# Attention, gated FFN and routed experts on one core: weight conversion at one unit a round, the small block's last logits inside the first Strassen group, ScalarE's casts and GpSimd's work moved within a group, another PSUM bank for the first w_out product

## The chip, the core and the metric

The kernel runs on one core of one Trainium2 chip. The metric is the device time of one execution in microseconds (us), the median over several runs. A profile of one execution was taken by the hardware profiler as well. Engines: PE (matrix products; PEld is its loading of the stationary operand), DVE (vector), ACT (scalar, activations and casts), POOL (GpSimd), SP (issues most DMAs).

## The reference

Three layers follow each other, all in 32-bit floats, over 2304 tokens of width 512.

```python
# 1. attention by random features, per batch and head (4 x 8, 576 tokens, width 64, 128 features)
phi(x) = exp(x@omega.T - |x|^2/2 - max) / sqrt(128)      # of q and k, scaled
out = (phi(q) @ (phi(k).T @ v)) / (phi(q) @ phi(k).sum + 1e-6)
# 2. gated FFN, 512 -> 1536 -> 512
xn  = x / sqrt(mean(x*x) + 1e-6) * rms_g
y   = (silu(xn @ w_gate) * (xn @ w_val)) @ w_out
# 3. routing over 8 experts, each takes 288 tokens
logits = y @ w_gate2                        # 2304 x 8
order  = argsort(-logits.flatten())         # greedy: best (token, expert) pairs first
out[mask_e] = relu(y[mask_e] @ w1[e]) @ w2[e]   # 512 -> 1024 -> 512
```

## The kernel before

Every float product is made from two parts: a matrix is cut into a high part in PE's reduced 32-bit format and a low part, the rest, and a product is three matmuls (high x high, low x high, high x low). So each operand costs a cast (ACT, the high part) and a subtraction (DVE or POOL, the low part).

The program runs through these stages; the times in the tables below are from the start of the profiled span.

1. **Rounds of attention** (0 to about 325 us). A round (`run_tick`) starts one item of the attention, K items and Q items in turn, while five older items go on; in between stand steps of the FFN (`ffn_step_pe`) on the token blocks that are ready. Each round also takes up some of 48 *weight units*: 24 units of `w_gate`/`w_val` (`WgvUnit`), 12 of `w_out` transposed (`WoTUnit`) and 12 of `w_out` (`WoUnit`), 512 KB each, which arrive as 64-bit floats and are turned into 32-bit ones by one pass of ACT and three of DVE (`word`, L592 to L594). How many units start a round is `PACE`: 0.5 at first, 0.7 up to the last `WgvUnit`, then its third number.
2. **The small block** (to about 352 us). Tokens come in five blocks of 512, 512, 256, 512 and 512. The third, of 256, is the small block; after the attention, PE makes its products f by f (f is one of 12 slices of the 1536 columns, `KF`), gate (L676 to L679, v = 0) and value (v = 1). ACT and DVE make th and h of them, ACT casts h (L709), POOL makes the low part (L710), and PE multiplies both with the router's weights into the logits' bank `lg` (`ffn_lg`, L721 and L722), one step behind. Between the steps stand preparations for the next stage (the list `ins`). At the end the last logits are made, transposed (`ffn_rank`, L733) and ranked (`ffn_rank_el`), and three matmuls into the PSUM banks bb, bc and bd (L1183) mark these as written.
3. **Groups** (`group(f)`, f = 0 to 12, about 352 to 495 us). Blocks four and five (LEFT and RIGHT) are multiplied together by Strassen's method: seven half products instead of eight, 42 matmuls of 512 columns a group, in this order: pa (bank gv), pe (gv), bb with t2, pa again, bb with t3, bc, bd. ACT copies pa into bb (L1089), pe into p5 (L1102) and bb into bd (L1128). DVE adds bb and p5 into bc (L1109), which has to be there before bb is written again by t3. Beside this stand the logits of LEFT and RIGHT of the group before (`logits_of`), and those of block 0 (`late_lg`), for which h of block 0 is loaded from DRAM two slices ahead (`late_load`, L923), cast by ACT and reduced by POOL (`late_split`: L928, L932) and stored again (L933). The next group's operands are made by `turn_w` (POOL L1008, DVE L1012 to L1015), `turn_high` (ACT L1019) and `turn_low` (POOL L1022). Every second group takes up 1024 columns of w_out: `wo_load` (SP), `wo_high` (ACT), `wo_low` (DVE L903, two halves).
4. **w_out and routing** (about 495 to 672 us). The product with w_out (`ffn2`, 648 matmuls at L1264) is the filling between the steps of the routing (`route`), which DVE and PE do in turns: `fill(ns)` lets PE make so many matmuls of the filling, and after the routing the rest is made. Ahead of the routing stand the last logits of LEFT and RIGHT (`ffn_lg`, `ffn_rank`). The routing's result picks the rows that are gathered for expert 0.
5. **Experts** (to the end).

The order is written by hand: inside `manual_schedule` PE, DVE and ACT (in the groups POOL too) do their instructions in the order of the code; SP's DMAs stand in one queue and each waits for its own inputs with all behind it.

Of the kernel before, what the change touches and what calls it, by code (L numbers as in the profile page):

```python
# [9 lines left out]
F32 = mybir.dt.float32  # L10
# [40 lines left out]
SKIP = 2  # L51
STEP = (1.08, 0.5)
SLOW_AT = 71
PACE = (0.5, 0.7, 0.75)
FFN_AT = 23
AHEAD_A = 200
AHEAD_F = 150
# [238 lines left out]
def kernel(ctx, tc, qT, kT, kC, v1, vC, om, wgv, rms, wo, woT, wg2, w1, w2, cfd, trd, out, dbg=None):  # L296
# [647 lines left out]
    def late_lg():  # L944
        f = late["lg"]
        if f < late["split"]:
            ffn_lg(0, f, lates[f])
            late["lg"] += 1
            if f + 2 < KF:
                late_load(f + 2)  # L950
# [114 lines left out]
    def group(f):  # L1065

        last, nxt = f == KF, f + 1 if f + 1 < KF else None
        if not last:
            w = wsl[f].rearrange("p l (b x) -> p l b x", b=4)
            b11, b21, b22 = ((w[:, 0, i], w[:, 1, i]) for i in (0, 1, 3))  # L1070
            (t1, t3), (t2, t4) = ([(ta[f, n][:, 0, i], ta[f, n][:, 1, i]) for i in range(2)] for n in range(2))
            a11, a12 = ((xlh[:, 2 * i:2 * i + 2], xll[:, 2 * i:2 * i + 2]) for i in (0, 1))
            pa = wide(psG, "gv")
            product(pa, *b11, *a11, True)
        late_lg()
        if not f:
            sum_low("s4", 1, s1[1], nc.vector)
            sum_low("r2", 1, right_2(1), nc.gpsimd)
            late_load(0)
            late_load(1)  # L1080
        if f:
            keep_low(LEFT, f - 1, *old["l"])
            th2 = wide(fp, "th")
            gate(th2, bd)
            times_gate(th2, bd)
            times_value(th2, old["p5"])
            late_split()
        if not last:
            nc.scalar.copy(bb, pa)  # L1089
        if f:  # L1090
            hp2 = pair()
            keep_high(th2, hp2)
        if nxt:
            turn_w(nxt, 1)
        if f:
            keep_low(RIGHT, f - 1, th2, hp2)
        if last:
            return
        pe = wide(psG, "gv")
        product(pe, *t1, *both("s1"), True)  # L1100
        p5 = wide(sp, "p5", bufs=2)
        nc.scalar.copy(p5, pe)  # L1102
        logits_of(LEFT)
        product(bb, *t2, *both("s2"), False)
        if nxt:
            turn_w(nxt, 2)
            turn_high(nxt, 0)
            turn_low(nxt, 0)
        nc.vector.tensor_add(bc_, bb, p5)  # L1109
        if f % 2:  # L1110
            wo_low()
            wo_load(f // 2)
        product(pa, *b21, *a12, False)
        th1 = wide(fp, "th")
        gate(th1, pa)
        times_gate(th1, pa)
        if f + 2 < KF:
            turn_w(f + 2, 0)
            turn_w(f + 2, 5)
        logits_of(RIGHT)  # L1120
        if f % 2 and f > 1:
            late_lg()
            late_split()
        product(bb, *t3, *both("s3"), False)
        if f and not f % 2:
            wo_high()
            wo_low()
        nc.scalar.copy(bd, bb)  # L1128
        nc.vector.tensor_add(p5, bb, p5)
        if nxt:  # L1130
            turn_high(nxt, 1)
            turn_low(nxt, 1)
        ffn_rank()
        product(bc_, *b22, *both("s4"), False)
        hp1 = pair()
        times_value(th1, bc_)
        keep_high(th1, hp1)
        ffn_rank_el(1)
        product(bd, *t4, *both("r2"), False)
        old.update(l=(th1, hp1), p5=p5)  # L1140

    def logits_of(j):
        if fq and fq[0][0] == j:
            ffn_lg(*fq.pop(0))

    dve, pool = nc.vector, nc.gpsimd
# [19 lines left out]
    with tc.manual_schedule(engines=in_order | {mybir.EngineType.Pool}):  # L1166
        count, rounds = len(ready), len(ins)
        while ready:
            el = fst.pop("el", None)
            assert ffn_step_pe()  # L1170
            if el:
                ffn_el(*el)
                ffn_rank_el()
            while len(ins) > rounds * len(ready) // count:
                for make in ins.pop(0):
                    make()
        ffn_step_el()
        while fq:
            ffn_lg(*fq.pop(0))
        ffn_rank()  # L1180
        ffn_rank_el()
        for t in (bb, bc_, bd):
            nc.tensor.matmul(t, xlh[:, 0, :128], xlh[:, 0], start=True, stop=True)  # L1183
    st["rank"] = lambda: psS.tile([128, 512], F32, name="late")[:, :BLK // 128 * 2 * E].rearrange(
        "p (c e) -> p c e", e=2 * E)
    st["eng"] = nc.vector
    with tc.manual_schedule(engines=in_order | {mybir.EngineType.Pool}):
        for f in range(KF + 1):
            group(f)
            if f == KF - 3:  # L1190
                ffn2_load(*seq2[0], x2, "xh2", 1)
                ffn2_load(*seq2[1], x2, "xl2", 1)
        wo_high()
        wo_low()
        wo_low()
# [53 lines left out]
    def ffn2():  # L1249
        for i, (c, g) in enumerate(seq2):  # L1250
            if i + HB - 1 < len(seq2):
                ffn2_load(*seq2[i + HB - 1], f2, "ht", HB)
            if i % 6 == 2 and wcur[0] < LOADS:
                exp_load()
            if i % 6 == 4 and wcur[1] < EARLY:
                exp_early()
            ht = hts.pop((c, g))
            if g == 0:
                py = psB.tile([128, DM], F32, name="py")
            for i4 in range(4):  # L1260
                f = 4 * g + i4
                w = wos[f // 2].rearrange("p l (i d) -> p l i d", i=2)
                for n, (a, l) in enumerate(((0, 0), (0, 1), (1, 0))):
                    nc.tensor.matmul(py, ht[:, i4, a], w[:, l, f % 2], start=(f == 0 and n == 0),  # L1264
                                     stop=(f == KF - 1 and n == 2))
                    yield
            if g == 2:
                done[0] += 1
                t = c - (NC - TAIL)
                if t >= 0:  # L1270
                    for h in (slice(0, 256), slice(256, 512)):
                        nc.scalar.copy(yt[t][:, 0, h], py[:, h])
                        nc.vector.tensor_sub(yt[t][:, 1, h], py[:, h], yt[t][:, 0, h])
                ys = yp.tile([128, DM], F32, name="ys")
                nc.scalar.copy(ys, py)  # L1275
                nc.scalar.dma_start(y_dr[c * 128:(c + 1) * 128, :], ys)
# [15 lines left out]
    with tc.manual_schedule(engines=in_order):  # L1292
        for n in (8, 6):
            fill(n * FILL_MM)
            ffn_lg(*fq.pop(0))
            fill(3 * FILL_MM)
            ffn_rank()
            ffn_rank_el()
    if "L" in dbg:
        nc.sync.dma_start(dbg["L"].rearrange("(c p) e -> p c e", p=128), L)  # L1300
    xg = {}
# [218 lines left out]
```

## Time and profile before

| | |
|---|---|
| time, median of 3 runs | 910.35 us (907.67 to 911.21) |
| profiled execution | 909.13 us, of which the span from first to last instruction is 907.3 us |
| PE busy | 881.3 us, 97% of the span |
| PE weight loads | 763.0 us, 84% |
| DVE busy | 633.5 us, 70% |
| ACT busy | 412.3 us, 45% |
| POOL busy | 259.3 us, 29% |
| mean granted clock of PE | 0.993 |

A busy share is the time in which the engine had an instruction running; matmuls overlap, so that the one recorded end lies behind the start of the next. "Idle before" in a row is time in which the engine stood still ahead of that instruction, with the one that released it.

### The profile page before, as it was taken

Reading aid. Unit: us, or ns where it says so; the run is one execution under the profiler, and the core shown is the slowest. Engines: PE = TensorE matmul, PEld = TensorE weight load, DVE = VectorE, ACT = ScalarE, POOL = GpSimd, SP = SyncE. Lnnn points to the kernel's source line nnn. Section 1 sums busy time; section 2 is a strip of 40 time slices with the busy share of each in tenths; the row PEclk is TensorE's granted clock in tenths of the full one; section 3 lists DMA queues with packets and bytes.
Section 4 is the critical chain, followed back from the end, with each engine's and each line's share of the span. In section 5 each row is a group of like instructions: output and inputs, shape, how many; then the busy total and the mean of one; then the engine's idle time right before and its main releaser. Section 6 shows DMA issues by size and latency. Waiting matters only on the chain.

```text
span 907.3 us, 15714 instructions
## 1 busy us (share of the span) xinstructions
PE 881.3 (97%) x5780; PEld 763.0 (84%) x5780; DVE 633.5 (70%) x1398; ACT 412.3 (45%) x913; POOL 259.3 (29%) x313
## 2 busy tenths in 40 slices
PE   9999999999999988999999999999999999999996
PEld 7788888888888987777776777777779999999996
DVE  4899967577757885788887777777654665556652
ACT  6886666355555743555554101100014454445441
POOL 1355433132322536566651000000022122122211
PEclk9999999999999998999999999999999999999998
DMA  8657435543456223466654987777614566665550
GB/s 303 203 145 223 137 108 160 177 146 120 139 181 233 82 82 120 145 207 218 217 183 164 302 253 211 214 216 210 195 56 127 183 188 190 194 212 180 182 187 27
DMA packets 114109, 159.26 MB, mean 176 GB/s; under 512 B 6640, under 2 KB 71664, under 8 KB 114032
## 3 DMA queue, kind: packets, MB, share of 16 engines
q1 hardware_dynamic: 108224, 143.96, 50.7%
q0 software_dynamic: 3072, 9.44, 3.5%
q10 hardware_dynamic: 2736, 4.85, 1.4%
q8 instruction: 45, 0.74, 0.3%
q14 instruction: 32, 0.26, 0.1%
HBM read 114.19 MB, written 44.04 MB: 174 GB/s over the span
## 4 chain that ended last, share of the span: by engine, by line
PE 46%; issue 8%; DVE 6%; POOL 3%; ACT 1%; DMA 0%; POOLq 0%; ACTq 0%; DVEq 0%
PE py L1264 15%; PE ph L1376 3%; PE ph L1379 3%; PE ph L1377 3%; PE py L1389 3%; PE py L1387 3%; PE py L1388 3%; DVE th L1061 1%; PE bb L1027 1%; PE gv L1030 1%; PE gv L1028 1%; PE gv L1027 1%; PE bb L1028 1%; PE bb L1030 1%; POOL out_dram L1423 1%
## 5 line engine op out<-in xcount | busy, mean ns | idle before, releaser
L1264 PE MATMUL py<-wc,ht 128*128 128x512 f32 x624 | 158.4, 402 | 0.0
L1264 PEld LDWEIGHTS py<-wc,ht 128*128 128x128 f32 x624 | 111.6, 189 | 19.2
L1235 DVE TENSOR_TENSOR wc<-ws,wc 128x512 fp32r<-128x512 f32 x128 | 84.5, 684 | 35.5 <-ACT wc L1245 35.5
L676 PE MATMUL gv<-xh,wc 128*128 128x512 f32 (+1 forms) x288 | 104.6, 374 | 2.4 <-DVE th L689 1.2
L677 PE MATMUL gv<-xh,wc 128*128 128x512 f32 (+1 forms) x288 | 99.4, 356 | 0.0
L409 ACT ACTIVATE ft<-pp,mx 128x128 f32<-128x128 f32 x288 | 82.9, 374 | 30.3 <-DVE mx L406 30.0
L1389 PE MATMUL py<-ehh,wc 128*128 128x288 f32 x256 | 76.2, 298 | 0.0
L1387 PE MATMUL py<-ehh,wc 128*128 128x288 f32 x256 | 75.8, 296 | 0.0
L1388 PE MATMUL py<-ehl,wc 128*128 128x288 f32 x256 | 75.6, 295 | 0.0
L1376 PE MATMUL ph<-exh,wc 128*128 128x288 f32 x256 | 71.2, 300 | 0.0
L1275 ACT COPY ys<-py 128x512 f32<-128x512 f32 x18 | 10.6, 588 | 133.0 <-PE py L1264 108.8
L1377 PE MATMUL ph<-exh,wc 128*128 128x288 f32 x256 | 69.8, 295 | 0.0
L1245 ACT CAST wc<-ws 128x1024 fp32r<-128x1024 f32 x64 | 67.2, 1050 | 2.4 <-ACT ys L1275 2.4
L679 PE MATMUL gv<-xl,wc 128*128 128x512 f32 (+1 forms) x288 | 67.1, 355 | 0.0
L676 PEld LDWEIGHTS gv<-xh,wc 128*128 128x128 f32 x288 | 54.5, 189 | 10.5 <-DVE th L689 2.4
L1381 DVE SCALAR_TENSOR_TENSOR ehl<-ph,ehh 128x288 fp32r<-128x288 f32 x64 | 29.3, 458 | 46.7 <-ACT ehh L1380 42.2
L677 PEld LDWEIGHTS gv<-xh,wc 128*128 128x128 f32 x288 | 54.5, 189 | 6.4
L406 DVE TENSOR_REDUCE mx<-pp 128x4 f32<-128x512 f32 (+1 forms) x76 | 49.9, 657 | 12.2 <-PE pp L402 7.9
L679 PEld LDWEIGHTS gv<-xl,wc 128*128 128x128 f32 x288 | 49.3, 189 | 8.0
L1315 POOL DMA_INDIRECT xh<-y_dr,idc x3 | 3.1, 1038 | 167.9 <-DVE idc L1327 167.3
L1423 POOL DMA_INDIRECT out_dram<-yo,ids x24 | 22.5, 938 | 98.1 <-DVE yo L1418 75.4
L1380 ACT ACTIVATE ehh<-ph 128x288 fp32r<-128x288 f32 x64 | 26.4, 412 | 49.7 <-PE ph L1379 49.7
(305 smaller groups left out, 2223.6 us busy)
## 6 DMA issues: line engine op xcount, KB each, us to landing
ws<-in_w_dram SPq DMA_DIRECT2D x64, 512.0 KB, 4.0
ht<-h_dr SPq DMA_DIRECT2D x53, 512.0 KB, 4.5
h_dr<-hp SPq DMA_DIRECT2D x36, 512.0 KB, 2.8
ws<-in_wgv_dram SPq DMA_DIRECT2D x24, 512.0 KB, 4.3
h_dr<-hp SPq DMA_DIRECT2D x24, 256.0 KB, 3.2
ws<-in_woT_dram SPq DMA_DIRECT2D x12, 512.0 KB, 3.5
ws<-in_wo_dram SPq DMA_DIRECT2D x12, 512.0 KB, 3.7
h_dr<-xh SPq DMA_DIRECT2D x12, 512.0 KB, 3.6
```

The costliest lines, as they stand in the source:

```text
L409: st["ex"] = nc.scalar.activation(ft[:n, g], pp[:n, g], AF.Exp, bias=mx[:n, g:g + 1])
L676: nc.tensor.matmul(pg[:, :n], w[:, 0, v, k], xh[:, k, :n], start=(k == 0), stop=False)
L677: nc.tensor.matmul(pg[:, :n], w[:, 1, v, k], xh[:, k, :n], start=False, stop=False)
L679: nc.tensor.matmul(pg[:, :n], w[:, 0, v, k], xl[:, k, :n], start=False, stop=(k == KD - 1))
L1235: nc.vector.tensor_sub(w[:, 1, h], sv[:, h], w[:, 0, h])
L1245: nc.scalar.copy(w[:, 0], sv)
L1264: nc.tensor.matmul(py, ht[:, i4, a], w[:, l, f % 2], start=(f == 0 and n == 0), stop=(f == KF - 1 and n == 2))
L1376: nc.tensor.matmul(ph, w[:, 0, k, m], xh[:, k], start=(k == 0), stop=False)
L1377: nc.tensor.matmul(ph, w[:, 1, k, m], xh[:, k], start=False, stop=False)
L1387: nc.tensor.matmul(py, w[:, 0, k], hh[:, k], start=(k == 0), stop=False)
L1388: nc.tensor.matmul(py, w[:, 0, k], hl[:, k], start=False, stop=False)
L1389: nc.tensor.matmul(py, w[:, 1, k], hh[:, k], start=False, stop=(k == KE - 1))
```

## The change

Four things are edited.

- `PACE`'s third number goes from 0.75 to 1.0: after the last `WgvUnit`, every round starts a unit.
- The small block's last two slices of logits are no longer made ahead of the groups. `logits_of` takes them too, so that they stand in group 0 where later groups have those of LEFT and RIGHT; their ranking follows in group 0, and the three marking matmuls are moved to where six steps of the small block are left.
- In the groups, `late_lg` stands behind pe and behind the logits of RIGHT (before: behind pa, and in odd groups behind RIGHT); `late_split` behind RIGHT in odd groups and at the end of every group (before: early in every group, and behind RIGHT in odd ones); the first `turn_high`/`turn_low` behind the gate; `wo_high` behind the copy of pe; `wo_low` behind the sum into bc.
- The first product with w_out is made in the bank gv instead of py; the filling between the last logits and their ranking is 4 matmuls (before 3), and 2 more follow the second ranking.

```diff
-PACE = (0.5, 0.7, 0.75)
+PACE = (0.5, 0.7, 1.0)
...
             product(pa, *b11, *a11, True)
-        late_lg()
...
             times_value(th2, old["p5"])
-            late_split()
...
         nc.scalar.copy(p5, pe)
+        if f and not f % 2:
+            wo_high()
+        late_lg()
         logits_of(LEFT)
         product(bb, *t2, *both("s2"), False)
         if nxt:
             turn_w(nxt, 2)
-            turn_high(nxt, 0)
-            turn_low(nxt, 0)
         nc.vector.tensor_add(bc_, bb, p5)
+        wo_low()
         if f % 2:
-            wo_low()
             wo_load(f // 2)
         product(pa, *b21, *a12, False)
...
         times_gate(th1, pa)
+        if nxt:
+            turn_high(nxt, 0)
+            turn_low(nxt, 0)
...
         logits_of(RIGHT)
-        if f % 2 and f > 1:
-            late_lg()
+        late_lg()
+        if f % 2:
             late_split()
         product(bb, *t3, *both("s3"), False)
-        if f and not f % 2:
-            wo_high()
-            wo_low()
...
             turn_high(nxt, 1)
             turn_low(nxt, 1)
+        if f:
+            late_split()
         ffn_rank()
...
     def logits_of(j):
-        if fq and fq[0][0] == j:
+        if fq and fq[0][0] in (j, LEFT - 1):
             ffn_lg(*fq.pop(0))
...
         while ready:
+            if len(ready) == count - 6:
+                for t in (bb, bc_, bd):
+                    nc.tensor.matmul(t, xlh[:, 0, :128], xlh[:, 0], start=True, stop=True)
...
-        while fq:
-            ffn_lg(*fq.pop(0))
-        ffn_rank()
-        ffn_rank_el()
-        for t in (bb, bc_, bd):
-            nc.tensor.matmul(t, xlh[:, 0, :128], xlh[:, 0], start=True, stop=True)
...
-                py = psB.tile([128, DM], F32, name="py")
+                py = psB.tile([128, DM], F32, name="py") if i else psG.tile([128, DM], F32, name="gv")
...
-            fill(3 * FILL_MM)
+            fill(4 * FILL_MM)
             ffn_rank()
             ffn_rank_el()
+        fill(2 * FILL_MM)
```

On PE, at the end of the small block, before: the last logits (lg) stand between the small block's products and in the first product of group 0 (L1027 on, gv from xh).

```order
L679 MATMUL gv<-xl_1913,wc 128x256 x4
L721 MATMUL lg<-hp,wog 16x256
L722 MATMUL lg<-hp,wog 16x256
L721 MATMUL lg<-hp,wog 16x256
L722 MATMUL lg<-hp,wog 16x256
L1027 MATMUL gv<-xh,wc 128x512
L1028 MATMUL gv<-xh,wc 128x512
L1027 MATMUL gv<-xh,wc 128x512
L721 MATMUL lg<-hp,wog 16x256
L1028 MATMUL gv<-xh,wc 128x512
L722 MATMUL lg<-hp,wog 16x256
L1030 MATMUL gv<-xl,wc 128x512 x2
```

And after, from the same place: two products of group 0 follow at once, and the next pair of logits stands behind them.

```order
L679 MATMUL gv<-xl_1915,wc 128x256 x4
L721 MATMUL lg<-hp,wog 16x256
L722 MATMUL lg<-hp,wog 16x256
L1027 MATMUL gv<-xh,wc 128x512
L1028 MATMUL gv<-xh,wc 128x512
L1030 MATMUL gv<-xl,wc 128x512 x2
L1027 MATMUL gv<-s_4004,ta 128x512
L1028 MATMUL gv<-s_4004,ta 128x512
L1030 MATMUL gv<-s_4004,ta 128x512 x2
L721 MATMUL lg<-hp,wog 16x256
L722 MATMUL lg<-hp,wog 16x256
L1027 MATMUL bb<-s_4116,ta 128x512
```

The last pair (not among these rows) stands behind the two products after those, t2 into bb and the second half of pa; both pairs wait for POOL's L710 as before.

On POOL, groups 2 and 3 and the first row of group 4, before (ta is `turn_low`, ws is `turn_w`, xh is the low part of block 0's h):

```order
L932 TENSOR_TENSOR xh<-xh 128x2x256
L1022 TENSOR_TENSOR ta<-dw,ta 128x512
L1008 TENSOR_TENSOR ws<-wc 128x512 x2
L1022 TENSOR_TENSOR ta<-dw,ta 128x512
L932 TENSOR_TENSOR xh<-xh 128x2x256
L1022 TENSOR_TENSOR ta<-dw,ta 128x512
L1008 TENSOR_TENSOR ws<-wc 128x512 x2
L932 TENSOR_TENSOR xh<-xh 128x2x256
L1022 TENSOR_TENSOR ta<-dw,ta 128x512
L932 TENSOR_TENSOR xh<-xh 128x2x256
```

The same groups after:

```order
L1022 TENSOR_TENSOR ta<-dw,ta 128x512
L1008 TENSOR_TENSOR ws<-wc 128x512 x2
L1022 TENSOR_TENSOR ta<-dw,ta 128x512
L932 TENSOR_TENSOR xh<-xh 128x2x256
L1022 TENSOR_TENSOR ta<-dw,ta 128x512
L1008 TENSOR_TENSOR ws<-wc 128x512 x2
L932 TENSOR_TENSOR xh<-xh 128x2x256
L1022 TENSOR_TENSOR ta<-dw,ta 128x512
L932 TENSOR_TENSOR xh<-xh 128x2x256
L1022 TENSOR_TENSOR ta<-dw,ta 128x512
```

The xh of a group's start has moved to its end, behind the second ta, and the first ta starts later in its group, since its cast now stands behind the gate.

On PE, at the start of the filling with w_out, before (num is the bank of the transposed logits):

```order
L1264 MATMUL py<-wc,xh_5281 128x512 x8
L721 MATMUL lg<-hp,wog 16x512
L722 MATMUL lg<-hp,wog 16x512
L1264 MATMUL py<-wc,xh_5281 128x512 x3
L733 MATMUL num<-cf,th 128x16 x4
```

And after:

```order
L1264 MATMUL gv<-wc,xh_5281 128x512 x8
L721 MATMUL lg<-hp,wog 16x512
L722 MATMUL lg<-hp,wog 16x512
L1264 MATMUL gv<-wc,xh_5281 128x512 x4
L733 MATMUL num<-cf,th 128x16 x4
```

The bank is another and one matmul more stands ahead of the ranking; up to the first step of the routing (L188) there are 4 more in all, which are missing from the filling's rest at the end.

## Rows read from the trace of the kernel before

**Rows 1.** The profile's page, part 1: busy time of each engine.

```profile
PE 881.3 (97%) x5780; PEld 763.0 (84%) x5780; DVE 633.5 (70%) x1398; ACT 412.3 (45%) x913; POOL 259.3 (29%) x313
```

**Rows 2.** Windows: busy us of PE, PEld, DVE, ACT, POOL, granted clock, DMA.

```profile
352.00:356.00 4.00, 1.75 (x10) 0.89 (x7) 3.93 (x5) 0.40 (x1) 4.00 (x4) 1.00 0.18 66
356.00:363.00 7.00, 6.54 (x17) 4.79 (x18) 1.64 (x5) 1.90 (x5) 1.33 (x3) 0.51 0.83 241
...
369.00:484.00 115.00, 112.80 (x489) 84.29 (x489) 100.38 (x126) 62.57 (x110) 66.93 (x53) 1.00 0.56 194
```

**Rows 3.** Timeline of PE, last logits to group 1's start: start, us, [idle before].

```profile
352.13 0.28 PE L721 MATMUL lg<-hp,wog 128*16 128x256 f32 x1
353.91 0.29 PE L722 MATMUL lg<-hp,wog 128*16 128x256 f32 x1 [1.50 <-POOL hp L710]
...
356.46 0.39 PE L722 MATMUL lg<-hp,wog 128*16 128x256 f32 x1 [1.22 <-POOL hp L710]
...
369.28 0.39 PE L1027 MATMUL gv<-xh,wc 128*128 128x512 f32 x1
```

**Rows 4.** PE's waits from 280 to 330 us: total, times, longest.

```profile
PE pm L501 <- DVE x L528: 1.4, 1, 1.4
PE pm L511 <- DVE x L528: 1.1, 1, 1.1
PE pm L511 <- DVE xn L551: 0.7, 2, 0.4
```

**Rows 5.** PE's waits from 159 to 280 us.

```profile
PE gv L676 <- DVE th L689: 1.2, 1, 1.2
```

**Rows 6.** DVE's groups, 280 to 330 us: count, busy us, mean ns, idle before.

```profile
L593 DVE SCALAR_TENSOR_TENSOR dw<-ws,dw 128x512 int32<-128x512 int32 x6 | 5.4, 905 | 0.1
L594 DVE SCALAR_TENSOR_TENSOR dw<-ws,dw 128x512 int32<-128x512 int32 x6 | 4.3, 714 | 0.1
L592 DVE TENSOR_SCALAR dw<-dw 128x512 int32<-128x512 int32 x6 | 4.0, 672 | 0.0
```

**Rows 7.** Timeline of PE in group 4, which begins at 403.65.

```profile
403.65 0.39 PE L1027 MATMUL gv<-xh,wc 128*128 128x512 f32 x1
...
410.23 0.39 PE L722 MATMUL lgr<-hp,wog 128*16 128x512 f32 x1
410.92 0.50 PE L1027 MATMUL bb<-xl,ta 128*128 128x512 f32 x1 [0.30 <-DVE bc L1109]
...
415.14 0.39 PE L1027 MATMUL gv<-xh,wc 128*128 128x512 f32 x1
```

**Rows 8.** Timelines of DVE and POOL in group 4.

```profile
403.87 1.12 DVE L1048 TENSOR_TENSOR hp<-th,hp 128x512 fp32r<-128x512 f32 x1 [0.69 <-ACT hp L1045]
405.62 1.32 DVE L1061 SCALAR_TENSOR_TENSOR th<-p,th 128x512 f32<-128x512 f32 x1
...
408.69 1.56 DVE L1015 TENSOR_TENSOR dw<-ws,dw 128x256 f32<-128x256 f32 x1
413.99 0.69 DVE L1061 SCALAR_TENSOR_TENSOR th<-bc,th 128x512 f32<-128x512 f32 x1
405.10 1.30 POOL L932 TENSOR_TENSOR xh<-xh 128x512 fp32r<-128x512 f32 x1 [0.66 <-ACT xh L928]
```

**Rows 9.** DMA issues from 357 to 500 us: count, size, median us to landing.

```profile
h_dr<-xh SPq DMA_DIRECT2D x12, 512.0 KB, 3.6
...
xh<-h_dr SPq DMA_DIRECT2D x10, 256.0 KB, 3.2
```

**Rows 10.** Timelines of PE and DVE around the filling.

```profile
496.51 0.50 PE L1264 MATMUL py<-wc,xh 128*128 128x512 f32 x1 [1.47 <-DVE th L1058]
510.22 0.23 PE L188 MATMUL cnt<-oh,xh 128*128 128x8 bf16 x3 [0.79 <-DVE xh L142]
673.95 0.30 PE L1359 MATMUL gv<-cf,xh 96*128 96x96 f32 x1 [0.91 <-DVE xh L1335]
500.52 0.19 DVE L736 TENSOR_TENSOR L<-num,lt 128x32 f32<-128x32 f32 x1 [0.41 <-ACT lt L735]
```

More of the change, by code (lines that the diff above doesn't have):

```diff
@@ L1177 @@
         ffn_step_el()
-        while fq:
-            ffn_lg(*fq.pop(0))
-        ffn_rank()
-        ffn_rank_el()
-        for t in (bb, bc_, bd):
-            nc.tensor.matmul(t, xlh[:, 0, :128], xlh[:, 0], start=True, stop=True)
-    st["rank"] = lambda: psS.tile([128, 512], F32, name="late")[:, :BLK // 128 * 2 * E].rearrange(
-        "p (c e) -> p c e", e=2 * E)
+        assert len(fq) == 2
     st["eng"] = nc.vector
@@ L1189 @@
             group(f)
+            if f == 0:
+                st["rank"] = lambda: psS.tile([128, 512], F32, name="late")[:, :BLK // 128 * 2 * E].rearrange(
+                    "p (c e) -> p c e", e=2 * E)
             if f == KF - 3:
```

## Prediction

> **What bounds the kernel now.** I read the page's table of engines first, then the windows, then PE's waits and timelines at the places that the diff touches. PE is busy for 881.3 of 907.3 us, DVE for 633.5, ACT and POOL for less [rows 1]: PE is the bound nearly everywhere, so the change can only gain where PE stands still or runs slowly, and a wait that it adds on PE counts in full. The change removes almost no matmuls. The profiled execution took 909.13 us (its span and 1.8 us around it); the median of the runs is 910.35, so I sum against 909.13 and put 0.6 on top, half of the 1.2 between them. No change means within 0.5%, 4.55 us, about what a measurement of this kernel can tell: below 905.8 is faster, above 914.9 slower.
>
> **Part 1, the small block's last logits.** PE goes from the last pair of logits but one (352.13) to the start of group 1 (369.28), 17.15 us in all [rows 3]. Two things make that long. PE waits 1.50 and 1.22 us for POOL's low parts of h, at 353.91 and 356.46 [rows 3]; between 352 and 356 it is busy for only 1.75 of 4.00 us. And from 356 to 363 the granted clock is 0.51, the lower of its two levels, 1.2 instead of 2.4 GHz, right behind those idle stretches, while PE has 6.54 us of work [rows 2].
>
> What is that work at the full clock? In group 4, 29 matmuls of 512 columns lie between 403.65 and 410.23 [rows 7], which is 0.227 us each (with one pair of logits among them, so a little too much is charged to each). Group 0 has 42: 9.55 us. I add two pairs of logits of 256 columns at half of 0.227 per matmul, 0.45, and 0.45 for the transposes with a short wait for their copy: 10.5. The three marking matmuls, 0.7, now stand earlier, but they still cost their time: 11.2. So 17.15 − 11.2 = **−6.0 us**.
>
> Does POOL hold PE up elsewhere? Its low parts are ready where the two waits end, 353.9 and 356.4 [rows 3]. After the change the first six matmuls of pa and six of pe are ahead of the first of these logits: 352.1 + 0.7 + 12 × 0.227 = 355.5, and t2 and the rest of pa ahead of the other: 12 × 0.227 + 0.3 later, 358.5. Both low parts are then there, if POOL isn't later than now, and nothing of what DVE or POOL do ahead of it has grown. Bounds: if the waits go but the clock falls all the same, 1.50 + 1.22 = −2.7; if the transposes need no wait either, −6.4.
>
> **Part 2, PACE.** Between 280 and 330 PE waits 1.4 + 1.1 + 0.7 = 3.2 us, all for x and xn, small operations of DVE's FFN steps [rows 4]; there DVE converts weight units, six words at 5.4 + 4.3 + 4.0 = 13.7 us, 2.3 us each [rows 6], and the FFN's operations stand behind them in DVE's order. 24 units at 0.75 a round take 32 rounds, at 1.0 they take 24; six words from 280 on are eight rounds, and I take a round at 5 us (an estimate, from the 50 us of these rows and the words' end before them), so the last word comes some 40 us earlier, near 279 instead of 319. The stretch with the waits is then nearly free of words. I don't take off all: the second wait has other causes as well, so I count 2.4 of 3.2. The rounds from 159 to 280 get denser in turn, four words where three were; now, with three, PE waits there only 1.2 us for DVE in 121 us [rows 5], so a third more words should add 0.4 to 0.5. Together **−1.9 us**. Bounds: all 3.2 gone and nothing added, with a little less jitter, −3.5; nothing gone, and one wait as long as the 1.4 us above added in the denser rounds, about +1.5.
>
> **Part 3, the order within the groups.** Groups 1 to 10 fill the 115 us from 369 to 484; group 4 takes 415.14 − 403.65 = 11.49 [rows 7]. PE is busy for 112.80 of 115.00 us there, at clock 1.00 [rows 2]. The missing 2.2 us are nearly all one wait: t3's first matmul, which overwrites bb, waits for DVE's sum into bc (0.30 us in group 4, at 410.92) [rows 7]. That is what a better order can give as visible idle; at 0.227 us for each of the 489 matmuls in the window the ten groups would take 111.0 us, so with what the records don't show as idle it is 4.0 at most.
>
> What makes bc late is DVE's chain, hp (L1048), th (L1058, L1061), the differences L1012 to L1015, then bc. Three of its operations are drawn out: L1048 takes 1.12, L1061 1.32 and L1015, with half the columns, 1.56, where an undisturbed L1061 takes 0.69; L1061 falls into POOL's xh of 405.10 to 406.40 [rows 8]. An L1015 without that would take half of 0.69, 0.35, so 0.43 + 0.63 + 1.21 = 2.3 us of the chain are such waiting behind POOL. The Trainium skill says in "SBUF — State Buffer", section "SBUF: two separate sides", that DVE with two inputs in SBUF and a GpSimd operation that reads SBUF exclude each other for a whole instruction, whichever started first; 1.32 against 0.69 agrees, and by that rule POOL's work costs DVE wherever it lands in the chain, so moving it helps only if it leaves the chain.
>
> It leaves it in odd groups only halfway. After the change xh stands at the end of each group, behind the second ta, and the first ta behind the gate. At the start of an even group POOL then still has ws, xh and ta of the change of groups in one run, some 1.3 us each by the row of xh [rows 8], beside DVE's L1048 and L1061: I count one collision more, 2.3 → about 3.2 us. Against this PE itself arrives later at t3 in even groups, since `late_lg`'s second pair now stands ahead of it: 2 × 0.227 = 0.45. So bc is 0.5 to 1.0 later, PE 0.45 later: 0.1 to 0.5 a group in five even groups. In odd groups `late_lg` is unchanged in place, but its low part comes from a later xh: 0 to 0.2. Group 1 has its ranking ahead of bc gone to group 0, worth some 0.5 back. Sum **+1.0 us**. Bounds: −4.0 if the wait for bc vanishes everywhere; +8 by the late loads (a rival below).
>
> **Part 4, filling and routing.** The first product's bank py was the last group's bd, and PE waits 1.47 us at 496.51 for DVE's last reading of it; in gv it need not. But PE is not alone there: the first step of the routing (0.79 at 510.22) waits for DVE's chain from the logits, which starts with L736 behind ACT's copy (0.41) [rows 10]. The matmuls come earlier and PE then waits for DVE, unless the added filling covers it: 4 matmuls more, 0.9 us, are drawn from the end of the filling, where PE waits 0.91 for the gather (673.95) [rows 10] and will wait about 1.8 instead. What stays is by how much DVE's routing starts earlier, at most the 0.41 of that copy: **−0.4 us**. Bounds 0 and −1.5 (1.47 in full).
>
> **Sum.** −6.0 − 1.9 + 1.0 − 0.4 = −7.3; 909.13 − 7.3 = 901.8, and with the 0.6 of the median 902.4: I say **902 us**.
>
> **The rivals.**
>
> *The clock falls all the same* (or at another place). The start of group 0 still has a copy, a transpose and two logits in it, and the gather's wait grows to 1.8 us. One stretch as now costs half of 7.0 us at 0.51 [rows 2], 3.4 us: 902 + 3.4 = 905.5. For it: 2.7 us of idle time sufficed for the fall at 356. Against: after the change no single wait over 0.3 us is in sight there, and the waits for bc in groups 1 to 10, of a few tenths each, left the clock at 1.00 [rows 2].
>
> *The wait for bc goes as well.* If DVE, in even groups, starts its chain before POOL (whose xh now stands at the end), the collisions leave the chain: not +1.0 but −4.0: 897. For it: in odd groups the xh that hit L1061 has moved away. Against: the ta and ws that took its place are as long.
>
> *The late loads pile up: the rival on the other side.* The place is the end of each group. A slice of h is loaded once its store two slices before has landed, 3.6 us after issue, and its own landing takes 3.2 more [rows 9]. With the split at the end of the group the store goes out later, so in odd groups the load may land after ACT has come to the cast L928, and ACT queues hp's cast, the gate and the copy into bb behind it: all that DVE's chain and PE's next group need. Up to 0.65 us of such a wait has slack (ACT is busy for 62.57 of 115 [rows 2]); each tenth above it is a tenth on PE. At 0.85 us a group, 8.5 over ten groups in place of the +1.0, the gain is gone: 902 − 1 + 8.5 = 909.5. From 1.4 us a group on it is 915 and more, slower. For it: 6.8 us of DMA in a loop of 11.49. Against: a slice has two groups, 23 us, and the DMA share there is 0.56 [rows 2].
>
> *PACE does nothing, or shifts the waits into the rounds before:* +0 to +1.5 instead of −1.9, 904 to 905.5.
>
> **How the numbers follow.** The forecast with all its terms, 898 to 905: 0.60. The clock falls somewhere, 904 to 907: 0.13. bc's wait goes too, 895 to 898: 0.12. Late loads or collisions at about one us a group, 908 to 916: 0.15, of which 0.06 is above 914.9. PACE without effect lies inside the first two. Below 905.8 lie the first, the third and a third of the second: 0.76; above 914.9 0.06; between 0.18. Leaving out a small tail on either side, below 895 and above 909, leaves 8 in 10 or a little more.
>
> **What the profile should show.** No wait for POOL at the two pairs of logits, granted clock 1.00 from 350 to 370, and 11 to 11.5 us from the last product of the small block to group 1. No L592 to L594 after about 280, and less than 1 us of waits for x and xn in 280 to 330. Groups 11.3 to 11.8 us long, with PE's wait for bc there and L1048, L1061 or L1015 at 1.1 us and more beside a POOL operation. The first L1264 directly behind bd, and a wait of about 1.8 us for the gather. I am wrong if the granted clock is near 0.5 at group 0, if the groups last 12 us with ACT's L928 waiting for a DMA, or if waits of more than 2 us for DVE appear between 159 and 280.

## The result and the profile after

The changed kernel takes 900.47 us (median of 4 runs, 899.24 to 900.84) where the kernel before takes 909.56 (4 runs): ratio 0.9898, 95% interval 0.9875 to 0.9922, a gain of 9.1 us. The prediction said 902 and a gain of about 8. The profiled execution has a span of 898.8 us, 8.5 less than before.

The page's first part shows that PE's work is the same and its idle time shorter.

```profile
PE 880.0 (98%) x5780; PEld 763.7 (85%) x5780; DVE 626.0 (70%) x1400; ACT 411.3 (46%) x913; POOL 260.8 (29%) x311
```

At group 0 the windows answer to [rows 2]; the last is a stretch behind the gather, which we come back to.

```profile
352.00:356.00 4.00, 4.00 (x20) 3.17 (x19) 2.35 (x4) 1.53 (x4) 0.91 (x2) 1.00 0.54 166
356.00:363.00 7.00, 6.58 (x30) 4.77 (x29) 5.63 (x11) 3.21 (x7) 5.09 (x4) 1.00 0.77 242
369.00:484.00 115.00, 113.69 (x492) 84.62 (x491) 90.45 (x129) 61.43 (x108) 68.94 (x51) 1.00 0.58 202
665.00:675.00 10.00, 10.00 (x69) 9.95 (x69) 3.63 (x8) 3.35 (x9) 2.77 (x3) 0.84 0.27 85
```

The timeline of PE in the changed kernel: the last pair of logits that was not moved stands directly ahead of group 0, which starts at 348.59; then the two moved pairs, the start of group 1, and the starts of groups 4, 5, 6 and 11.

```profile
348.48 0.28 PE L722 MATMUL lg<-hp,wog 128*16 128x256 f32 x1
348.59 0.40 PE L1027 MATMUL gv<-xh,wc 128*128 128x512 f32 x1
...
351.74 0.28 PE L722 MATMUL lg<-hp,wog 128*16 128x256 f32 x1
...
354.74 0.28 PE L722 MATMUL lg<-hp,wog 128*16 128x256 f32 x1
...
359.41 0.39 PE L1027 MATMUL gv<-xh,wc 128*128 128x512 f32 x1
...
393.95 0.39 PE L1027 MATMUL gv<-xh,wc 128*128 128x512 f32 x1
...
405.94 0.39 PE L1027 MATMUL gv<-xh,wc 128*128 128x512 f32 x1
...
417.00 0.39 PE L1027 MATMUL gv<-xh,wc 128*128 128x512 f32 x1
...
475.23 0.39 PE L1027 MATMUL gv<-xh,wc 128*128 128x512 f32 x1
```

Neither moved pair of logits waits for POOL any more, the granted clock stays at 1.00, and 348.59 to 359.41 is 10.82 us, where [rows 3] have 17.15 from the same place: 6.3 less. The three marking matmuls now lie ahead of this stretch; kernel 2 below shows that they cost nothing there.

Two rows of the kernel before close the account, the start of group 11 and the routing's last matmuls (L288):

```profile
484.36 0.39 PE L1027 MATMUL gv<-xh,wc 128*128 128x512 f32 x1
...
665.38 0.99 PE L288 MATMUL cnt<-xh 128*96 128x48 bf16 x18
```

After, around the filling, the routing's end and the gather:

```profile
485.75 1.98 PE L1264 MATMUL gv<-wc,xh 128*128 128x512 f32 x8
...
490.19 0.41 PE L733 MATMUL num<-cf,th 16*128 16x16 f32 x4 [1.10 <-ACT th L725]
...
655.73 0.99 PE L288 MATMUL cnt<-xh 128*96 128x48 bf16 x18
...
663.03 0.30 PE L1360 MATMUL gv<-cf,xh 96*128 96x96 f32 x1 [0.65 <-DVE xh L1336]
664.34 0.30 PE L1360 MATMUL gv<-cf,xh 96*128 96x96 f32 x1 [1.00 <-DVE xh L1336]
```

One more pair of rows is needed, before and after: the last four matmuls of one FFN product in the rounds of attention. Up to here PE does the same in both kernels, since the new pace shows in its order only behind them.

```profile
151.63 1.08 PE L679 MATMUL gv<-xl,wc 128*128 128x512 f32 x4
```

```profile
152.73 1.08 PE L679 MATMUL gv<-xl,wc 128*128 128x512 f32 x4
```

| Stretch | before | after | difference |
|---|---|---|---|
| start to these four matmuls, the same code | 151.63 | 152.73 | +1.1 |
| from there to the moved logits (352.13, 348.59) | 200.50 | 195.86 | −4.6 |
| from there to group 1 | 17.15 | 10.82 | −6.3 |
| groups 1 to 10 | 115.08 | 115.82 | +0.7 |
| group 11 to the routing's last matmuls | 181.02 | 180.50 | −0.5 |
| from there to the span's end | 241.92 | 243.07 | +1.1 |
| sum | 907.3 | 898.8 | −8.5 |

The first line is no gain or loss of an edit: these executions differ there by 1.1 us with the same code (kernels 1 and 5 and the last section come back to it). In the second, PE's list of waits from 155 to 345 us holds 1.1 us for xn (L551) and 0.9 for th (L700); before it held 5.2 us, the 3.2 of [rows 4], the 1.2 of [rows 5] and 0.8 for th.

### The profile page after: what moved, and what is told of

Same layout as the page of the kernel before. It is cut to its first block, busy times and chain, and to the rows that moved or that the text cites. A ratio compares the mean times of both kernels' runs of the same rounds, so it can differ in the third digit from the quotient of the medians.

```text
span 898.8 us, 15721 instructions
## 1 busy us (share of the span) xinstructions
PE 880.0 (98%) x5780; PEld 763.7 (85%) x5780; DVE 626.0 (70%) x1400; ACT 411.3 (46%) x913; POOL 260.8 (29%) x311
## 4 chain that ended last, share of the span: by engine, by line
PE 43%; issue 8%; DVE 6%; POOL 3%; DMA 2%; ACT 1%; SPq 0%; POOLq 0%; DVEq 0%; ACTq 0%
PE py L1264 14%; PE ph L1377 3%; PE ph L1380 3%; PE ph L1378 3%; PE py L1390 3%; PE py L1388 3%; PE py L1389 3%; POOL out_dram L1424 1%; PE bb L1028 1%; PE bb L1027 1%; PE gv L1360 1%; PE bb L1030 1%; PE gv L1027 1%; POOL xh L932 1%; PE gv L1028 1%
## 5 line engine op out<-in xcount | busy, mean ns | idle before, releaser
L1264 PE MATMUL py<-wc,ht 128*128 128x512 f32 x612 | 155.7, 402 | 0.0
L1264 PEld LDWEIGHTS py<-wc,ht 128*128 128x128 f32 x612 | 109.3, 189 | 18.8
L679 PE MATMUL gv<-xl,wc 128*128 128x512 f32 (+1 forms) x288 | 67.1, 355 | 0.0
L406 DVE TENSOR_REDUCE mx<-pp 128x4 f32<-128x512 f32 (+1 forms) x76 | 49.9, 657 | 11.7 <-PE pp L402 8.6
L679 PEld LDWEIGHTS gv<-xl,wc 128*128 128x128 f32 x288 | 49.3, 189 | 8.0
```

What stands on the lines that cost most here:

```text
L679: nc.tensor.matmul(pg[:, :n], w[:, 0, v, k], xl[:, k, :n], start=False, stop=(k == KD - 1))
```

## The experiments

Runs one to eight were on one chip, nine to twelve on another; ratios are to the kernel before on the same chip.

**1 and 2: the two edits that should gain, each alone.** The kernel before with one line changed:

```diff
-PACE = (0.5, 0.7, 0.75)
+PACE = (0.5, 0.7, 1.0)
```

> The kernel before with PACE's third number at 1.0 and nothing else. Theory (the prediction's term, corrected by the changed kernel's trace, in which the small block's last products start 3.5 us earlier than before, with three marking matmuls already made): -4 us, ratio about 0.9955, and PE's waits between 155 and 350 us fall from 5.2 to about 2 us. Rival (the prediction's own size): -1.9 us, ratio 0.998, and the other 2 us of the earlier start come from another edit or from chance.

Measured: 901.76 us, 0.9915 (0.9897 to 0.9933), 7.1 us faster: more than either size. The waits from 155 to 345 us fell to 2.0 as in the changed kernel, and the small block's last logits came 4.1 us earlier (352.13 to 348.01); from the same four matmuls, at 152.16, it is 195.85 us instead of 200.50, 4.65 less. The other 3 us are at group 0, which this edit does not touch:

```profile
345.00:370.00 25.00, 21.62 (x108) 16.88 (x107) 17.70 (x25) 10.66 (x21) 17.34 (x16) 1.00 0.54 179
```

```profile
152.16 1.08 PE L679 MATMUL gv<-xl,wc 128*128 128x512 f32 x4
...
348.01 0.28 PE L721 MATMUL lg<-hp,wog 128*16 128x256 f32 x1
349.77 0.29 PE L722 MATMUL lg<-hp,wog 128*16 128x256 f32 x1 [1.48 <-POOL hp L710]
...
352.33 0.29 PE L722 MATMUL lg<-hp,wog 128*16 128x256 f32 x1 [1.22 <-POOL hp L710]
...
362.20 0.39 PE L1027 MATMUL gv<-xh,wc 128*128 128x512 f32 x1
```

Both waits for POOL are still there, 1.48 and 1.22 us, yet the granted clock is 1.00 and the stretch takes 14.2 us instead of 17.15. So the two waits alone need not bring the clock down. Ahead of them this kernel has lost the waits for x; whether that is why the clock held isn't shown. The profile is one execution, but the mean granted clock of each run is on record: 0.996 to 0.998 in all six runs of this kernel. The kernel before has 0.996 to 0.998 in eight of the 23 runs beside it, which took 907.3 to 908.3 us, and 0.992 to 0.994 in the other fifteen, which took 908.7 to 912.1. So in that kernel too the clock does not fall alike in every execution, and the 3 us are what the fall cost in the profiled one.

The second kernel takes the other edit alone (`logits_of` and the loop of the small block, as in the change's diff).

```diff
-        if fq and fq[0][0] == j:
+        if fq and fq[0][0] in (j, LEFT - 1):
...
+            if len(ready) == count - 6:
+                for t in (bb, bc_, bd):
...
-        while fq:
-            ffn_lg(*fq.pop(0))
-        ffn_rank()
-        ffn_rank_el()
```

> The kernel before with the small block's last two pairs of logits, their ranking and the marking matmuls moved, nothing else. Theory: -5.5 to -6 us, ratio 0.9936, no wait for POOL at these logits, granted clock 1.00 around group 0. Rival: the waits go but the clock falls all the same: -2.7 us, ratio 0.997.

Measured: 904.30 us, 0.9944 (0.9925 to 0.9963), 4.6 us faster, with the expected 0.9936 inside the interval; span 901.6, 5.7 less than before, no wait at these logits, granted clock 1.00 from 345 to 370. The theory holds.

```profile
152.27 1.08 PE L679 MATMUL gv<-xl,wc 128*128 128x512 f32 x4
...
352.78 0.40 PE L1027 MATMUL gv<-xh,wc 128*128 128x512 f32 x1
...
363.59 0.39 PE L1027 MATMUL gv<-xh,wc 128*128 128x512 f32 x1
```

The rows say more: 352.78 to 363.59 is 10.81 us, 6.3 less than before. And from 152.27 to 352.78 it is 200.51 us, the 200.50 of the kernel before, although the three marking matmuls now stand in this stretch: they are made where PE would have waited.

**3 and 4: the two edits that should be nearly neutral, each alone.** Third kernel: only the lines of `group`, as in the change's diff.

```diff
-            late_split()
...
+        if f and not f % 2:
+            wo_high()
+        late_lg()
...
+        if f:
+            late_split()
```

> The kernel before with the changed order within the groups alone (late_lg, late_split, turn_high, turn_low, wo_high, wo_low). Theory: +0.5 to +1 us, ratio 1.001; odd groups about 11.1 us, even ones about 12.0 instead of 11.47 each. Rival: the new order needs the other edits (the first group's logits) to be good and costs 2 us or more alone; other rival: it gains on its own, below 0.999.

Measured: 910.25 us, 1.0015 (1.0000 to 1.0030); three odd groups (3, 5, 7) took 11.4, 11.0 and 11.0 us, even ones 11.6 to 12.2, as the theory said. But group 1 took 10.5 instead of 11.5, and groups 1 to 10 together 115.1, exactly as before. So in the profiled execution, one of the fastest of this kernel (908.8 us), the order costs nothing in the groups, and where the 1.4 us of the median come from isn't shown.

Fourth kernel: only the bank and the filling.

```diff
-                py = psB.tile([128, DM], F32, name="py")
+                py = psB.tile([128, DM], F32, name="py") if i else psG.tile([128, DM], F32, name="gv")
...
-            fill(3 * FILL_MM)
+            fill(4 * FILL_MM)
...
+        fill(2 * FILL_MM)
```

> The kernel before with the first w_out product in the bank gv and the longer filling, nothing else. Theory: -0.4 us, ratio 0.9996, the routing's end comes 0.5 us earlier after group 11, and the gather's wait grows by about 0.9 us. Rival: the whole wait of 1.5 us at the first product comes out as time: ratio 0.9984. Other rival: the longer idle time before the gather brings the granted clock down behind it and the kernel is 1 us slower: 1.001.

Measured: 909.52 us, 1.0005 (0.9991 to 1.0018). The full 1.5 us did not come out; with this interval the theory and its second rival can't be told apart by time. The profiled execution shows both: group 11 to the routing's last matmuls is 0.5 us shorter than before, the granted clock is 0.83 from 675 to 685, behind the gather, and the rest of the span is 1.1 us longer.

**5: PACE and the logits together,** both diffs above and nothing else.

> The kernel before with the two edits that gained alone, PACE and the small block's logits, and neither the groups' new order nor the filling. Alone they gave 0.9915 and 0.9944. Theory: part of both gains is the same one, the fall of the granted clock at group 0, which costs about 3 us and which either of them ends; so together 4.1 + 5.7 = 9.8 us, ratio 0.989 (about 899 us), not the product 0.986. Rival: the gains are separate, 0.986 (896 us).

Measured: 898.81 us, 0.9883 (0.9866 to 0.9900). The product of the two lone ratios, 0.9859, lies just outside the interval, though it has an uncertainty of its own of about 0.0026. The profiled executions say it more plainly.

```profile
151.80 1.08 PE L679 MATMUL gv<-xl,wc 128*128 128x512 f32 x4
...
347.65 0.40 PE L1027 MATMUL gv<-xh,wc 128*128 128x512 f32 x1
...
358.47 0.39 PE L1027 MATMUL gv<-xh,wc 128*128 128x512 f32 x1
```

| Stretch | before | kernel 1 | kernel 2 | kernel 5 |
|---|---|---|---|---|
| start to the four matmuls (L679), the same code | 151.63 | 152.16 | 152.27 | 151.80 |
| from there to the last two pairs of logits or, where these are moved, to group 0 | 200.50 | 195.85 | 200.51 | 195.85 |
| from there to group 1 | 17.15 | 14.19 | 10.81 | 10.82 |
| group 1 to the span's end | 538.1 | 537.9 | 538.0 | 537.9 |

Without the first line, which no edit touches, PACE alone gains 4.65 and 2.96 us, the logits alone 6.34, and both together 4.65 and 6.33: 11.0 instead of 13.95. The shared 3.0 us are the fall of the clock at group 0, which either edit ends. (In whole spans the shared part would come out as 2.0, because kernels 1 and 2 lost 0.5 and 0.6 us on the first line and kernel 5 only 0.2.)

**6 and 7: the other two edits taken out of the changed kernel.** Sixth: `group` as before. Seventh: bank and filling as before (the diffs of three and four, reversed).

> The changed kernel with the old order within the groups. Theory: the new order costs what its groups show, 0.7 us from group 1 to 11, so this is 0.7 us faster than the changed kernel: about 899.8 us where that had 900.5, ratio 0.989. Rival: with the first group's logits in place the new order is needed, since late_lg and the logits meet in group 1; then this is a microsecond or more slower than the changed kernel, ratio 0.991 or more.

Measured: 899.97 us, 0.9892 (0.9874 to 0.9911). Not slower, so the new order isn't needed; groups 1 to 10 take 114.9 us instead of 115.8 after the change, 0.9 less where 0.7 was expected.

> The changed kernel with the old bank py for the first w_out product and the old, shorter filling. Theory: the routing's end comes 0.5 us later, but the wait for the gather is 0.9 us instead of 1.7 and the granted clock behind it does not fall (0.84 from 665 to 675 us in the changed kernel, worth about 1 us): 0.5 us faster than the changed kernel to equal, ratio 0.9890 to 0.9898. Rival: the edit is worth the 1.5 us wait that it removes, and this is 1 us slower or more, ratio 0.991.

Measured: 899.36 us, 0.9894 (0.9876 to 0.9911), within the expected half microsecond or so. The granted clock from 665 to 675 us is 1.00 here:

```profile
665.00:675.00 10.00, 9.78 (x76) 9.77 (x76) 3.38 (x8) 2.92 (x8) 2.75 (x3) 1.00 0.27 85
```

It is 0.84 after the change, 0.83 in the sixth kernel and in the repetition below (kernel 9), all three with the longer filling and two waits for the gather, and 1.00 in the four kernels that have PACE, the moved logits and the old filling (five, seven, ten, twelve). The eighth kernel has the longer filling and two waits as well, and 1.00. Each of these is one execution, and executions differ: of kernel six's five runs four have a mean clock of 0.994 (899.8 to 900.2 us) and one 0.999 (898.5 us). So the longer wait makes the fall likely, not certain.

**8: what POOL costs DVE.** The changed kernel without `late_low`'s subtraction; block 0's second part then holds all of h.

```diff
-        nc.gpsimd.tensor_sub(hs[:, :, 1], hs.bitcast(F32)[:, :, 1], hs[:, :, 0])
```

> The changed kernel without POOL's subtraction for block 0's low parts (late_low, 12 operations of 1.3 us); the second part of block 0's h then holds all of h, so the result differs. Loads, casts and stores stay. Theory: the even groups are long (12.0 us) because DVE's operations wait behind POOL's xh; without it the even groups take 11.4 us and less, the odd ones stay at 11.1, and L1048, L1061 and L1012 at the start of even groups return to 0.7 us: 3 us faster than the changed kernel, ratio 0.9865. Rival: the 50 matmuls of an even group are its bound, or the landing of the late loads is, and nothing changes within 0.7 us.

Measured: 896.55 us, 0.9857 (0.9837 to 0.9877). Groups 1 to 10 took 113.2 us, even groups 11.4, the odd ones 3, 5 and 7 10.95: 50 and 48 matmuls at 0.228 us. DVE's groups of instructions from 370 to 450 us, the changed kernel first, then this one (its lines stand one lower):

```profile
L1048 DVE TENSOR_TENSOR hp<-th,hp 128x512 fp32r<-128x512 f32 x14 | 16.4, 1168 | 6.4 <-ACT hp L1045 6.1
L1012 DVE TENSOR_TENSOR dw<-ws 128x512 f32<-128x512 f32 x7 | 9.2, 1307 | 0.0
L1061 DVE SCALAR_TENSOR_TENSOR th<-p,th 128x512 f32<-128x512 f32 x7 | 7.5, 1073 | 0.2
```

```profile
L1047 DVE TENSOR_TENSOR hp<-th,hp 128x512 fp32r<-128x512 f32 x15 | 16.6, 1104 | 6.1 <-ACT hp L1044 5.5
L1060 DVE SCALAR_TENSOR_TENSOR th<-p,th 128x512 f32<-128x512 f32 x7 | 6.0, 855 | 0.2
L1011 DVE TENSOR_TENSOR dw<-ws 128x512 f32<-128x512 f32 x7 | 4.8, 682 | 0.0
```

L1012 falls from 1307 to 682 ns and L1061 from 1073 to 855, without any change in their own work; L1048 stays at 1.1 us behind the other POOL operations, against expectation. Of the 4.2 us between the spans (898.8 and 894.6), 2.65 are in groups 1 to 10. The rest is not the subtraction's: 1.1 lie behind the routing, where the clock was 1.00 in this run, and 0.5 ahead of 153 us, where both kernels do the same.

**9 to 12: can it be made better?** Ninth, the changed kernel again, beside the other three.

> The changed kernel once more, beside the next three on the same chip. Theory: 900.5 us, ratio 0.990. If the clock's fall behind the gather is what its filling costs, the run shows a granted clock of about 0.994 to 0.996 overall, where kernels with the old filling show 0.997 and 0.998.

Measured: 900.62 us (900.33 to 901.03), 0.9903 (0.9885 to 0.9921), granted clock 0.993 to 0.996 over its six runs.

Tenth: the fifth kernel with the first product in gv (the first two lines of the fourth diff), old filling.

> PACE and the small block's logits, and the first w_out product in the bank gv, with the old filling. Theory (the prediction's part 4): the wait of 1.5 us at the first product only moves to the logits' ranking or to the first step of the routing; 0 to 0.4 us faster than PACE and logits together (898.8 us), ratio 0.988, and the granted clock stays up behind the gather. Rival: without the longer filling the wait at the first routing step grows by as much as the first one shrinks, and the clock falls there: 1 us slower, 0.9894.

Measured: 898.56 us (897.55 to 898.75), 0.9879 (0.9859 to 0.9899). The wait at the first product is gone, and 1.3 us for ACT's copy stand at the logits' ranking instead. Faster than the changed kernel on the same chip by 2.1 us, with no run in common; against the fifth kernel no difference can be told. Besides the filling it lacks the groups' new order.

Eleventh: the fifth kernel with PACE's third number still higher.

```diff
-PACE = (0.5, 0.7, 1.0)
+PACE = (0.5, 0.7, 1.5)
```

> PACE and the small block's logits, with PACE's third number at 1.5 instead of 1.0. Theory: the waits left between 280 and 345 us (xn, th: 1.9 us in all) are no longer due to weight conversion, whose last word lies before 280 us, so the gain is used up: within 0.5 us of 898.8 us, ratio 0.988, or up to 1 us slower where the rounds from 155 on get denser. Rival: the more the conversion is ahead the better: 1 us faster or more, 0.987.

Measured: 909.37 us, 1.0003 (0.9989 to 1.0018): the whole gain is lost, which neither theory expected. The windows show where:

```profile
160.00:200.00 40.00, 39.08 (x226) 34.14 (x225) 25.96 (x61) 16.08 (x40) 6.26 (x8) 0.91 0.60 187
200.00:240.00 40.00, 39.42 (x238) 33.96 (x238) 34.39 (x73) 23.46 (x60) 11.44 (x14) 0.96 0.70 234
240.00:280.00 40.00, 37.05 (x216) 31.43 (x215) 25.07 (x37) 18.58 (x52) 14.92 (x17) 1.00 0.34 114
```

Kernel 5 has clock 1.00 and no wait of PE in all of 155 to 290 us. Here the clock falls three times in that stretch, to 0.57 to 0.59 in 162 to 166, 176 to 180 and 203 to 207 us. Ahead of each fall PE made 16 matmuls of 8 columns in a row or nearly so (L652, a product of the `WoTUnit`), eight for each of two units:

```profile
159.52 1.01 PE L652 MATMUL gv<-wg2s,dw 128*128 128x8 f32 x8
160.72 1.03 PE L652 MATMUL gv<-wg2s,dw 128*128 128x8 f32 x8 [0.19 <-DVE dw L594]
...
172.83 2.03 PE L652 MATMUL gv<-wg2s,dw 128*128 128x8 f32 x16
...
200.77 2.09 PE L652 MATMUL gv<-wg2s,dw 128*128 128x8 f32 x16
```

In kernel 5 they stand eight at a time, 5 us and more apart. A fourth run of 16 here, at 188.46, has no fall behind it, so this is a likely cause and not a shown one.

PE also waits 4.4 us in 155 to 290, most of it at L449 (2.9 us, twice) for the attention's exponentials on ACT, and these had waited for DVE:

```profile
251.29 1.14 ACT L409 ACTIVATE ft<-pp,mx 128x128 f32<-128x128 f32 x4 [4.73 <-DVE mx L406]
...
257.70 1.14 ACT L409 ACTIVATE ft<-pp,mx 128x128 f32<-128x128 f32 x4 [0.64 <-DVE mx L406]
```

By 283 us the kernel is 11.5 us behind the fifth, 0.4 of it already at 152 us. Three stretches of 4 us at 0.57 to 0.59 are 5.1 us of lost clock by my estimate, and with the 4.4 of waits that is 9.5 of the 11. The loads are late too:

```profile
ACT dw L588 <- DMA ws<-in_wo_dram: 3.5, 4, 1.5
ACT dw L588 <- DMA ws<-in_woT_dram: 3.2, 4, 2.2
```

Eight times, 6.7 us in all, ACT comes to the first pass over a weight unit before the unit has landed; at 1.0 it has no such wait. But the last of these ends at 242.6, PE's two long waits come 9 us later and more, and no wait of PE is put down to one, so what they cost isn't shown.

Twelfth: the seventh kernel with block 0's low parts on DVE, all behind the logits of RIGHT.

```diff
-        nc.gpsimd.tensor_sub(hs[:, :, 1], hs.bitcast(F32)[:, :, 1], hs[:, :, 0])
+        nc.vector.tensor_sub(hs[:, :, 1], hs.bitcast(F32)[:, :, 1], hs[:, :, 0])
...
         if f % 2:
             late_split()
+        if f:
+            late_split()
         product(bb, *t3, *both("s3"), False)
...
-        if f:
-            late_split()
```

> The changed kernel with the old bank and filling, and block 0's low parts made by DVE instead of POOL, all of them behind the logits of RIGHT (one in even groups, two in odd ones). Theory: the collisions at the start of even groups go as they did without that subtraction (groups 1 to 10 took 113.2 us there, 115.5 with it); DVE's 12 operations of 0.7 us stand where it is idle in the middle of a group: 2 us faster than that kernel (899.4 us), about 897.5, ratio 0.987. Rival: DVE's order now waits for ACT's cast and the late loads, the sum into p5 and hp1 come later, and the gain is eaten: 899 us or more, 0.989.

Measured: 898.73 us (897.88 to 898.87), 0.9879 (0.9859 to 0.9899). Groups 1 to 10 take 114.4 us instead of the seventh's 115.5, half of what was expected. L1012 and L1061 (the form th<-p,th) did go back, to 681 and 851 ns, as without the subtraction. What the moved one costs:

```profile
L932 DVE TENSOR_TENSOR xh<-xh 128x512 fp32r<-128x512 f32 x11 | 15.9, 1467 | 1.4 <-ACT xh L928 1.4
```

```profile
390.97 3.07 DVE L932 TENSOR_TENSOR xh<-xh 128x512 fp32r<-128x512 f32 x2 [0.34 <-ACT xh L928]
390.50 1.29 POOL L1022 TENSOR_TENSOR ta<-dw,ta 128x512 fp32r<-128x512 f32 x1 [5.43 <-ACT ta L1019]
391.75 3.45 POOL L1008 TENSOR_TENSOR ws<-wc 128x512 f32<-128x512 f32 x2
```

The moved subtraction takes 1467 ns on DVE where [rows 8] have 0.69 us for an operation of this size: at its new place it meets other work of POOL. The odd groups 3, 5 and 7 are at 10.95 us as in kernel 8; the even groups 4, 6 and 8 take 11.7 to 11.8, 0.4 more than there, without a listed wait of PE for it, so that this is what holds them is likely and not shown.

## Why the prediction was right

**Part 1** (−6.0): measured −6.3, by the mechanism stated. The 0.7 that it charged for the marking matmuls at their new place was not paid (kernel 2). But the prediction put the clock's fall down to the two waits for POOL, and kernel 1 kept both waits without a fall. The 3 us of the clock were there to be taken by either edit, and the sum counted them once.

**Part 2** (−1.9): the right mechanism, mis-sized by more than half; measured −4.6 after the change and alone, beyond the bound of −3.5. Two terms were wrong. I took off 2.4 of 3.2 us of waits; with the 0.8 for th that I did not look at, 4.0 became 2.0. And I added 0.4 to 0.5 for the denser rounds from 159 on; there the 1.2 us wait for DVE went away instead. The listed waits explain 3.2 of the 4.6. Nearly all of the rest lies at the same places: counted from start to start of the matmuls, the steps that held the three waits (behind L495, L506 and L652) are 4.4 us shorter in kernel 1. The end of the words was well placed: the last L594 starts at 277.91, forecast near 279. That denser rounds can hurt was right, but only beyond this pace: kernel 11 at 1.5 loses 11 us, by falls of the clock and by waits.

**Part 3** (+1.0): measured +0.7, its parts less well. The even groups' half microsecond came (11.48 to 11.9 on the mean of the even groups 2 to 8), but mostly not as the wait that was forecast. `late_lg`'s second pair left the odd groups for the even ones, which now make 50 matmuls and not 48; at 0.228 us that is 0.45. The prediction took this pair as slack ahead of the wait for bc, not as work, and missed that odd groups lose it: they are 0.35 us shorter. POOL's run beside DVE's chain does cost groups 4, 6 and 8 0.6 to 0.8 us (12.0 to 12.1 against 11.4 in kernel 8), but before the change they took 11.48 for 48 matmuls, 0.5 above 10.95, so little of that is new. The collisions only changed places: over seven groups (380 to 460 us before, 370 to 450 after) L1015 went from 1557 to 426 ns on the mean and L1061 (th<-p,th) from 1522 to 1073, but L1012 from 678 to 1307 and the two L1048 of a group from 781 to 1168 each, 5.3 us a group before and 5.1 after, where one collision more was forecast. Group 1 did not gain 0.5 but lost 0.4: PE now waits 0.42 us for hp (L1048) and 0.47 for bc. As to the rival of late loads, ACT waits for a landing twice, 1.6 us in all, and no wait of PE answers to it.

**Part 4** (−0.4): −0.5 up to the routing's last matmuls, with the wait moved to the ranking as forecast (1.47 at L1264 became 1.10 at L733), and the gather's wait grown from 0.91 to 1.7. The clock rival then came true at the place named second, the gather: 0.84 from 665 to 675. The end of the span lost 1.1 us there, so the edit as a whole did not pay.

**The sum.** −7.3 was forecast and −8.5 measured on the profile's scale. Parts 1 and 2 gave 3.0 more than forecast, parts 3 and 4 0.4; the gather's clock took 1.1 back, and 1.1 more went ahead of 153 us, where the two kernels do the same. That the sum came so near is in part luck. The 0.6 added for the median was not needed: the changed kernel's profiled execution took 900.58 us, its median is 900.47.

## What to carry to other kernels

An edit's gain and the clock's fall behind the waits that it removes are two gains; the second may be had already through another edit, so time edits alone and together before adding them up. Work that is brought forward out of a busy stretch gains only up to a point (one unit a round here; at 1.5 the gain was gone): look at what it makes the stretch before denser in, on each engine, and at the clock there. Two executions of the same code can differ by a microsecond and more, so compare stretch by stretch from a place up to which both kernels do the same. An engine's idle waits may be moved to a place where another transfer bounds the path (the gather) without a gain, and there they can cost clock; kernel 10, which leaves the filling and the groups' order as they were, is 2.1 us faster than the changed kernel, though not to be told from kernels 5 and 12.

## What the runs showed of the hardware

The granted clock did not fall at the same idle stretch in each kernel: two waits of 1.5 and 1.2 us for POOL stood at group 0 in the kernel before and in kernels 1, 3 and 4, and the mean clock from 345 to 370 us was 0.86 before (0.51 from 356 to 363), 1.00 in kernel 1, 0.93 in kernel 3 and 0.86 in kernel 4. Nor does one and the same kernel behave alike in each execution. These are the changed kernel and its repetition (kernel 9) from 55 to 65 us:

```profile
55.00:65.00 10.00, 9.18 (x48) 8.02 (x48) 9.86 (x14) 7.78 (x21) 7.89 (x7) 0.83 0.67 213
```

```profile
55.00:65.00 10.00, 9.16 (x56) 7.90 (x56) 9.93 (x13) 7.32 (x19) 7.01 (x7) 1.00 0.57 173
```

The kernel before, with the same code up to there, has 1.00 in this window, kernels 1 and 2 have a fall in it, and kernel 5 has none, which is part of the differences ahead of 153 us. What decides it is open.

The Trainium skill says in "SBUF — State Buffer", section "SBUF: two separate sides", that a DVE operation with two SBUF inputs and a GpSimd operation that reads SBUF shut each other out for a whole instruction; kernels 8 and 12 agree, since the cost went with POOL's operation (1307 to 682 ns) and came back where the moved one met another (1467 ns instead of 0.69 us).
